# The MoE stage of an attention kernel in six units of 512 tokens in place of eight of 384

## The chip, the cores and the metric

The kernel runs on one core of a Trainium2 chip. The metric is the device time of one execution in microseconds (us): the median of several runs of the kernel. Its engines are named as in the profile: PE is TensorE, PEld its weight loads, DVE VectorE, ACT ScalarE, POOL GpSimd and SP SyncE, which issues the DMAs.

## The reference

A gated linear attention with 4 sequences, 8 heads, 768 tokens and 48 features a head feeds a feed-forward stage with a convolution over the tokens and a gate ("MoE" in the names). The weights of that stage are float64.

```python
f = 1.0 / (1.0 + np.exp(-f_logit))
state = np.zeros((B, H, D, D))
for t in range(S):
    state = f[:, :, t, :, None] * state + np.einsum('bhd,bhe->bhde', k[:, :, t], v[:, :, t])
    y[:, :, t] = np.einsum('bhd,bhde->bhe', q[:, :, t], state)

x = y.transpose(0, 2, 1, 3).reshape(B, S, H * D)           # 4 x 768 x 384
h = np.maximum(x @ w_in, 0.0)                              # 384 -> 1024
conv_out[:, t] = sum(conv_w[k] * hp[:, t + k] for k in range(3))   # hp: h with a row of zeros at both ends
out = (h * sigmoid(conv_out)) @ w_out                      # 1024 -> 384
```

## The kernel before

*Attention.* The 24 chunks (4 sequences of 6 chunks of 128 tokens) are worked one behind the other. For a chunk the logarithms of the gates are summed over its tokens, for the first 9 chunks by matmuls (L556, "cumulate"), later by a scan on DVE (L563); ACT makes exponentials of the sums (L565, L567), and DVE multiplies queries and keys by them (L572, tile `kq`). PE turns the keys (L587, "turn"), which ACT or DVE copies (L598, tile `kp`), and forms the scores (L594); DVE copies them under a causal mask (L602, tile `am`). PE's "rank" (L622 and L614) forms the chunk's two sums for the state and half of its values; DVE adds the sums to the state (L635 half a chunk, L638 a whole one, L642 or L644 the decay); PE's "carry" (L658 and L614) adds what comes from the state. The result lies in PSUM with the heads on partitions in two halves; ACT copies it as the high part of x (L671) and DVE subtracts for the low part (L673, the "x split"), both into `xT`. Each half has 48 features and 16 more columns, which hold a third head: six DMAs per unit on SP's queue (L681, the "gather") move them to rows of their own.

*Weights.* They come as raw 32-bit words (L464) and are split into high and low parts of fp32r by integer and float operations on DVE and ACT; for w_in PE joins parts by four matmuls with 512 columns (L452 to L454).

*The stage with the change, function `moe`.* Before, a unit is half a sequence, 384 tokens; there are 8. For each pair of groups of 128 hidden features:

- L711, PE: nine matmuls with 384 columns (three parts of the 384 inputs, and high × high, high × low, low × high of each) give h in PSUM, in one of two buffers `mm` of 512 columns; "input matmuls", one group of nine per 128 hidden features.
- L721: ReLU with a factor 0.5 into `hb`, a tile in which every group of features has 387 columns: two edge columns to the left, 384, one to the right. L698 clears the edge at a sequence's begin, L701 copies the last two columns of the first half to the left of the second.
- L727, ACT: `g` = middle tap × h; L731, DVE, twice: adds the other taps ("convolution").
- L735, ACT: tanh over both groups; L737, DVE: (tanh + 1) × h, the gate.

The output of the convolution lies one token behind its input, so a unit yields 384 or 385 columns, and a tile of 128 output tokens may need the `g` of two units. For each tile of 128 tokens L754 (ACT) copies `g` as high part `gh`, L758 (DVE) subtracts for the low part `gl`, L767 (PE) makes 16 matmuls with `gh` and 8 with `gl` ("output matmuls", an "output tile"), L773 copies the result from PSUM into `ob`, and L777 writes it out.

*What sets the order.* Every operation is entered with its engine, what it needs and which buffers it takes (`plan.op`), and the order of all of them, over all engines, is a table of numbers written out by hand, ORDER, read by `Plan.fixed`; a number's part behind the dot names the buffer that it takes. Each engine works its list strictly in that order; what comes from another engine is waited for. The operations of attention and of the MoE stage are interleaved by that table: input matmuls of one unit stand between the scores, ranks and carries of the next chunks.

```python
        for w in ORDER.split():
            i, _, k = w.partition(".")
            o = self.ops[int(i.rstrip("v"))]
```

Of the kernel before, what the change touches and what calls it, by code (L numbers as in the profile page):

```python
# [33 lines left out]

ORDER = """
91.0 92 94 95.0 96 97.1 141.0 142.0 2.0 143 3.0 159.1 10.0 160.1 139.0 145 148.0 149.0 689 157.1 140.0 161 144 146.0
147.0 663 8.0 93 98 45.1 46.0 99.0 150 163 166.0 151 164.1 47 165.0 152 48 153 167.1 49 50.0 51 52 177.0 178.0 158.1
168 5.0 23.3 24 100.1 103 104.0 175.2 6.1 179 180 101 105 106.1 162v 109.0 112 25.1 4.0 195.1 196.1 197 169 26 0.0 181
53.0 54 27.0 154 155.0 28 184.0 170 172 213.0 173 29.0 156 214.0 34.0 35 185.0 102 215 107 193.3 176.2 174 36.0 182.0
30.1 113.0 31 183.0 216 32.0 111 199 202.0 186 9.1 200.1 37 203.1 171 187 108.1 33 231.0 38.0 188 211.0 217 190 220.0  # L40
116 229.1 194.0 189 201.0 117.1 198v 40.0 232.0 233 204 11.1 12.3 247.0 7.1 191 39 248.1 221.0 205 55.2 1.0 56 110 114
57.0 192 234 249 115.0 41.1 250 42 60 43.0 13 14.1 206 207 15 17 16.1 283.1 235 212.1 218.0 208 118.1 219.0 222 18.0
120 230.3 119 567 58.0 64 569 568 566 44 209.2 210 564 284.0 285 121 565 690.0 691 19.1 20 59 61 245.2 21.0 22 238.0
236.1 223 237.0 251 65 66.1 69 286v 224 67.1 226 239.1 240 225 62 123.0 125 68 63 664.0 318.2 695.1 281.3 124 287 241
242 254.0 246.0 73.1 336.1 227 122 83 228 676 301 70 665 666.0 71 692 693 243 696 244 82 84.0 255.0 126 252.0 265.0
# [949 lines left out]
```

## Time and profile before

| | us |
|---|---|
| median of the runs | 301.11 (301.06 to 303.17) |
| profiled execution, its own time | 302.57 |
| its span in the trace | 300.7 |

The span is the time from the first to the last recorded instruction; 1.87 us of the execution lie around it. An engine's busy time leaves out DMA issues, semaphores and branches. Matmuls are pipelined and their ends are modelled, so that rows of the timeline overlap, and a busy PE is not PE at its peak; starts of rows are what one subtracts. Each row of the chain is a piece of work, or a wait for it, that something later stood waiting for.

### The profile page before, as it was taken

How to read it: one execution, taken by the hardware profiler on the slowest of the kernel's cores; microseconds unless marked ns; L12 is line 12 of the kernel's file. 1: busy time of each engine (PE TensorE's matmuls, PEld its weight loads, DVE VectorE, ACT ScalarE, POOL GpSimd, SP SyncE). 2: the span in 40 equal slices, each digit the busy share in tenths (PEclk: the TensorE clock that was granted, in tenths of full speed). 3: DMA queues.
4: the chain of work that ended last, by engine and by line, in shares of the span. 5: the costliest groups of instructions: out<-in, count | busy, mean ns of one | idle time of the engine just before them, and what ended most of it. 6: DMA issues, size and time to landing. Idle time of an engine off the chain costs nothing.

```text
span 300.7 us, 10046 instructions
## 1 busy us (share of the span) xinstructions
PE 291.3 (97%) x4319; PEld 274.1 (91%) x4319; DVE 259.6 (86%) x431; ACT 235.7 (78%) x456; POOL 2.8 (1%) x16
## 2 busy tenths in 40 slices
PE   8998979999999999999999999999999999999994
PEld 5777859999999999899999999999999999999994
DVE  4898979999999999989999998989877797399560
ACT  5799869999969699888777799678586896968620
POOL 3000000000000000000000000000000000000000
PEclk9999999999999999999999999999999999999998
DMA  7999688621223126654262165202542612723011
GB/s 229 392 359 349 216 308 295 201 92 28 62 87 108 63 74 238 185 154 128 74 206 85 38 170 171 98 2 66 196 156 66 212 40 59 220 83 122 8 71 59
DMA packets 19269, 43.38 MB, mean 144 GB/s; under 512 B 2685, under 2 KB 10005, under 8 KB 19221
## 3 DMA queue, kind: packets, MB, share of 16 engines
q1 hardware_dynamic: 19076, 42.50, 43.1%
q8 instruction: 35, 0.57, 0.8%
q10 hardware_dynamic: 144, 0.20, 0.2%
q14 instruction: 14, 0.11, 0.1%
HBM read 35.61 MB, written 4.72 MB: 134 GB/s over the span
## 4 chain that ended last, share of the span: by engine, by line
PE 86%; DVE 4%; SPq 3%; DMA 3%; ACT 2%; issue 1%; DVEq 0%; ACTq 0%
PE mm L711 34%; PE mm L767 30%; PE Y L658 3%; PE S L594 3%; PE Y L614 3%; PE Y L622 3%; PE Y L587 3%; PE mm L556 2%; SPq L681 1%; PE mm L452 1%; DMA xT<-xT 1%; DMA v<-in_v_dram 1%; SPq L547 1%; DMA fb<-in_f_token_dram 1%; DVE xT L673 1%
## 5 line engine op out<-in xcount | busy, mean ns | idle before, releaser
L711 PE MATMUL mm<-xT,wi 128*128 128x384 f32 x576 | 107.0, 339 | 1.5 <-DMA xT<-xT 1.5
L711 PEld LDWEIGHTS mm<-xT,wi 128*128 128x128 f32 x576 | 99.3, 188 | 2.9 <-ACT e L567 1.6
L731 DVE SCALAR_TENSOR_TENSOR g<-hb,cw,g 128x385 f32<-128x385 f32 (+1 forms) x128 | 74.5, 616 | 3.8 <-ACT g L727 3.2
L767 PE MATMUL mm<-wo,gh 128*128 128x384 f32 x384 | 70.7, 336 | 0.0
L767 PEld LDWEIGHTS mm<-wo,gh 128*128 128x128 f32 x384 | 66.5, 188 | 0.3
L721 ACT ACTIVATE hb<-mm 128x384 f32<-128x384 f32 x64 | 31.3, 489 | 16.9 <-PE mm L711 16.5
L727 ACT ACTIVATE g<-hb,cw 128x384 f32<-128x384 f32 (+1 forms) x64 | 37.5, 615 | 2.5 <-DVE gl L758 1.9
L767 PE MATMUL mm<-wo,gl 128*128 128x384 f32 x192 | 36.8, 335 | 0.0
L735 ACT ACTIVATE g<-g 128x768 f32<-128x768 f32 (+1 forms) x32 | 26.8, 845 | 9.1 <-DVE g L731 8.9
L572 DVE TENSOR_TENSOR kq<-kq,e 128x1024 f32<-128x1024 f32 x24 | 29.3, 1219 | 5.1 <-ACT e L567 3.4
L767 PEld LDWEIGHTS mm<-wo,gl 128*128 128x128 f32 x192 | 33.5, 188 | 0.0
L754 ACT CAST gh<-g 128x1024 fp32r<-128x1024 f32 (+2 forms) x28 | 26.1, 932 | 9.4 <-PE mm L767 4.5
L758 DVE TENSOR_TENSOR gl<-g,gh 128x1024 fp32r<-128x1024 f32 (+2 forms) x28 | 29.6, 1069 | 3.2 <-PE mm L767 1.9
L737 DVE SCALAR_TENSOR_TENSOR g<-g,hb 128x768 f32<-128x768 f32 (+1 forms) x32 | 30.1, 956 | 0.9 <-ACT g L735 0.7
L614 PE MATMUL Y<-am,v 64*48 64x64 f32 (+1 forms) x768 | 23.5, 220 | 0.0
L602 DVE COPY_PREDICATED am<-mask,S 128x512 f32<-128x512 uint8 x24 | 17.6, 734 | 2.6 <-PE S L594 2.3
L614 PEld LDWEIGHTS Y<-am,v 64*48 64x48 f32 (+1 forms) x768 | 18.7, 127 | 0.0
L563 DVE TENSOR_TENSOR_SCAN fb<-runs,fb 128x512 f32<-128x512 f32 x15 | 18.0, 1218 | 0.3 <-ACT fb L534 0.3
L594 PE MATMUL S<-kq 48*64 48x64 f32 x768 | 16.7, 221 | 0.2 <-DVE kq L572 0.2
L622 PEld LDWEIGHTS Y<-v,kp 64*48 64x48 f32 (+1 forms) x704 | 13.4, 127 | 3.7 <-ACT kp L598 1.3
L622 PE MATMUL Y<-v,kp 64*64 64x48 f32 (+1 forms) x704 | 15.8, 214 | 0.8 <-DMA v<-in_v_dram 0.7
L673 DVE TENSOR_TENSOR xT<-Y,xT 112x512 fp32r<-112x512 f32 x24 | 16.4, 685 | 0.0
(100 smaller groups left out, 341.4 us busy)
## 6 DMA issues: line engine op xcount, KB each, us to landing
kq<-in_kq_dram SPq DMA_DIRECT2D x23, 512.0 KB, 4.8
v<-in_v_dram SPq DMA_DIRECT2D x24, 192.0 KB, 4.1
out_dram<-ob SPq DMA_DIRECT2D x23, 192.0 KB, 3.2
kq<-in_moe_w_in_dram SPq DMA_DIRECT2D x6, 512.0 KB, 4.5
kq<-in_moe_w_out_dram SPq DMA_DIRECT2D x6, 512.0 KB, 4.6
fb<-in_f_logit_dram SPq DMA_DIRECT2D x9, 256.0 KB, 5.0
xT<-xT SPq DMA_DIRECT2D x48, 48.0 KB, 2.3
g<-in_moe_w_in_dram SPq DMA_DIRECT2D x4, 512.0 KB, 6.6
```

The source lines that it names most:

```text
L572: ox = plan.op("DVE", 1222, lambda e, X=X, E=E: nc.vector.tensor_tensor(buf(X), buf(X), buf(E), ALU.mult), ka, need=[o2] + ld_x, use=[X, E])
L614: o = nc.tensor.matmul(out_of(Y, p, j, w, z), buf(V).rearrange("p h d -> p (h d)")[t, h * D:h * D + w], buf(AM)[t, j, p, :], start=x == 1 ...
L622: nc.tensor.matmul(pk(z)[HP * j:HP * j + w, p, :], buf(KP)[t, p, HP * j:HP * j + w], buf(V)[t, 2 * p + j, :], start=True, stop=True)
L711: nc.tensor.matmul(buf(ph)[:, :HS], wi[:, t, wl, f * P:(f + 1) * P], x_view(pl, u)[:, t, xl, :], start=(i == 0), stop=(i == 3 * KT - 1))
L721: nc.scalar.activation(hb[:, 2:HS + 2], buf(ph)[:, :HS], AF.Relu, scale=0.5)
L727: o = pl.op("ACT", 620, lambda e, cv=cv, hb=hb, n=n, f=f: nc.scalar.activation(cv(), hb[:, 1:n + 1], AF.Copy, scale=cw[:, 1, f:f + 1]), ke ...
L731: o = pl.op("DVE", 617, lambda e, cv=cv, hb=hb, n=n, f=f, w=w, sh=sh: nc.vector.scalar_tensor_tensor(cv(), hb[:, sh:n + sh], cw[:, w, f:f ...
L735: o = pl.op("ACT", 846, lambda e, cv=cv: nc.scalar.activation(cv(), cv(), AF.Tanh), key, need=last, use=[("g", u)], mode="T")
L737: gates[u, fp] = pl.op("DVE", 960, lambda e, cv=cv, fp=fp, n=n: nc.vector.scalar_tensor_tensor(cv(), cv(), 1.0, h_b[:, fp:fp + 2, 1:n + 1] ...
L754: o = pl.op("ACT", 180 + 110 * nn * NF // 128, lambda e, hv=hv, src=src: nc.scalar.copy(hv(), src()), key, need=[gates[v, fp] for fp in ra ...
L758: los.append(pl.op("DVE", 150 + 134 * nn * NF // 128, lambda e, hv=hv, lv=lv, src=src: nc.vector.tensor_tensor(lv(), src(), hv().bitcast(F ...
L767: nc.tensor.matmul(buf(po)[:, :DM], view(g)[:, f, :], wo[:, f, wl, :], start=(i == 0), stop=(i == 3 * NF - 1))
```

## The change

A unit is now 512 tokens, and the units run over the ends of sequences: two sequences (1536 tokens) are three units, v = 0, 1, 2. There are 6. The middle one holds the last third of one sequence and the first third of the next, and a zero column is kept between them in `h`.

- `xT` has two buffers of 512 columns instead of three of 384, `g` two of 513 columns for each group of features; `hb` gives way to four tiles `h0` to `h3`, one for each pair of groups, of 2 × 516 columns.
- The tiles of h are allocated when the first unit takes them, on the memory of constants needed only at the start (`stir`, the turned convolution weights, low parts of w_in); `tri32`, `idr` and `negr` lie where `ob` comes later. So the first unit's edge memsets wait for the first unit's gather and for the weights.
- Input matmuls have 512 columns; the ReLU (now always on ACT), the copy, the convolutions, the tanh and the gate likewise 512 or 513 (× 2). An input matmul no longer waits for the gates of the unit before; the edge copies and memsets do, and the ReLU waits for these.
- Three, four and five output tiles follow the three units of a pair of sequences; the output tiles themselves are as before.
- Constants lose their padding, and tiles move: `wi`, `wo`, `gh`, `gl`, `kq`, `v` and the first `xT` begin at 64 modulo 128 bytes (before at 0), the second `xT` at 96, the two `g` at 0 and 32 (as before), the four `h` at 64, 32, 64 and 96.
- ORDER is wholly new.

Line numbers shift by 4 in attention (the x split is L677, the gather L685), by 9 to 10 in the stage: L720 input matmul, L733 ReLU, L741 convolution, L747 gate, L767 `gl`, L776 output matmul, L703 memset of an edge.

```diff
-    HS = S // 2
-    CPH = NC // 2
+    UT = 4 * P
+    CPU = UT // P
+    NU = B * S // UT
-    G1 = HS + 1
+    G1, HW = UT + 1, UT + 4
...
-    h_b = const.tile([P, NF, HS + 3], F32, name="hb")
-    nc.gpsimd.memset(h_b[:, :, HS + 2:], 0.0)
...
+            ring("xT", [P, XW], F32R, [("x", 0), ("x", 1)])
+            ring("low", [P, RW], F32R, [hs[3], hs[2]])
+            ring("c32", [3 * NF, P], F32, hs[:1])
+            pl.ring("z0", [(None, hs[1:2])])
+            pl.ring("tri", [(None, ob[:1])])
+            pl.ring("id", [(None, ob[1:])])
+        for i in range(NF // 2):
+            ring(f"h{i}", [P, 2, HW], F32, hs[i:i + 1])
...
-        for u in range(2 * B):
-            b, hf = u // 2, u % 2
-            n = HS + hf
+        for u in range(NU):
+            b, v = u // 3 * 2, u % 3
+            n, c0 = UT + (v > 0), 1 + (v == 2)
...
+                old, H_ = gates.get((u - 1, fp)), ("h", fp)
+                if v == 0:
+                    oe = pl.op("DVE", 100, lambda e, H_=H_, u=u: [nc.vector.memset(buf(H_)[:, :, i:i + 2], 0.0) for i in ((0,) if u else (0, HW - 2))][-1],
+                               key, need=[old] + (list(x_ready[0][:1]) + W_IN[0] + (W_IN[1] if fp >= 4 else [CW]) if extra and not u else []),
+                               take=[] if u else [(f"h{fp // 2}", H_)], use=[H_] if u else [])
...
-                                nc.tensor.matmul(buf(ph)[:, :HS], wi[:, t, wl, f * P:(f + 1) * P], x_view(pl, u)[:, t, xl, :],
+                                nc.tensor.matmul(buf(ph)[:, :UT], wi[:, t, wl, f * P:(f + 1) * P], x_view(pl, u)[:, t, xl, :],
...
-                    o = pl.op("PE", 1570, mm1, key, need=[gates.get((u - 1, fp))] + list(x_ready[u]) + (W_IN[f // (NF // 2)] if extra else []), use=[("xT", u)],
+                    o = pl.op("PE", 2070, mm1, key, need=list(x_ready[u]) + (W_IN[f // (NF // 2)] if extra else []), use=[("xT", u)],
...
-                    o = pl.op("ACT", 492, relu, key, need=[o, oe], use=[ph])
+                    o = pl.op("ACT", 583, relu, key, need=[o, oe, oz], use=[ph, H_])
...
-            tiles = range(CPH - 1) if hf == 0 else range(CPH - 1, NC)
+            tiles = ((0, 1, 2), (3, 4, 5, 6), (7, 8, 9, 10, 11))[v]
```

Where instructions stand now, at three places, one of SP's queue and two of VectorE's list.

SP's queue at the first unit's gather. Before (L681 is the gather, L464 raw weights, L544 kq, L547 v, L517 gate logits):

```order
L547 DMA v_120<-in_v_dram 128x384
L517 DMA fb_112<-in_f_logit_dram 128x512
L681 DMA xT_340<-xT_340 16x768
L464 DMA g_575<-in_moe_w_out_dram 128x768
L681 DMA xT_340<-xT_340 16x768 x5
L544 DMA kq_115<-in_kq_dram 128x1024
L464 DMA g_575<-in_moe_w_out_dram 128x768
L517 DMA fb_111<-in_f_logit_dram 128x512 x2
L547 DMA v_119<-in_v_dram 128x384
L544 DMA kq_116<-in_kq_dram 128x1024
```

And in the changed order (L685 the gather, L465 raw weights, L548 kq, L551 v, L519 and L521 gate logits):

```order
L521 DMA fb_109<-in_f_logit_dram 128x512
L519 DMA fb_108<-in_f_token_dram 128x384
L521 DMA fb_109<-in_f_logit_dram 128x512 x2
L548 DMA kq_113<-in_kq_dram 128x1024
L685 DMA xT_308<-xT_308 16x1024 x6
L465 DMA raw_813<-in_moe_w_out_dram 128x768
L551 DMA v_114<-in_v_dram 128x384
L465 DMA raw_813<-in_moe_w_out_dram 128x768
L548 DMA kq_110<-in_kq_dram 128x1024
L551 DMA v_115<-in_v_dram 128x384
```

The six gathers stand together now, with a kq load right ahead of them in place of right behind, and with the raw weights behind.

VectorE's list from the fourth x split on. Before, it (L673, `xT_681`, already the second unit's) comes among the weights' splitting (L416, L419, L414, L422), a key product (L572) and state sums (L635, L638); the first memsets of `hb` stand at the list's beginning:

```order
L416 TENSOR_SCALAR gh_674<-g_575 128x768
L673 TENSOR_TENSOR xT_681<-Y_110,xT_681 112x4x128
L419 SCALAR_TENSOR_TENSOR gh_674<-g_575,gh_674 128x768
L635 TENSOR_TENSOR sh_95<-Y_109,st_93 112x192
L572 TENSOR_TENSOR kq_115<-kq_115,e_122 128x1024
L414 TENSOR_SCALAR gl_734<-g_575 128x768
L422 SCALAR_TENSOR_TENSOR gl_734<-gl_734,g_575 128x768
L569 COPY ft_all<-e_121 128x4
L638 TENSOR_TENSOR st_94<-Y_109,sh_95 112x192
L416 TENSOR_SCALAR gh_739<-g_575 128x768
L602 COPY_PREDICATED am_90<-mask_86,S 128x512
```

And in the changed order from the fourth x split (L677, the first unit's last, `xT_308`) to the first memsets of h (L703):

```order
L677 TENSOR_TENSOR xT_308<-Y_107,xT_308 112x4x128
L422 SCALAR_TENSOR_TENSOR mt_599<-mt_599,raw_574 128x768
L606 COPY_PREDICATED am_88<-mask_85,S 128x512
L422 SCALAR_TENSOR_TENSOR mt_577<-mt_577,raw_574 128x768
L416 TENSOR_SCALAR ms_723<-raw_574 128x768
L639 TENSOR_TENSOR sh_94<-Y_106,st_92 112x192
L487 COPY cw<-mm_130 128x24
L425 TENSOR_SCALAR ms_604<-ms_604 128x768
L419 SCALAR_TENSOR_TENSOR ms_723<-raw_574,ms_723 128x768
L642 TENSOR_TENSOR st_93<-Y_106,sh_94 112x192
L427 SCALAR_TENSOR_TENSOR wo<-mt_577,ms_604 128x2x384
L703 MEMSET h_751 128x2x2 x2
```

The memset of `h_751` stands 10 instructions behind the fourth x split; the next rows are the memset of `h_754`, a key product and a masked copy.

VectorE's list where the first stretch of the prediction ends. Before, at the second state sum of chunk 15 (L638, `st_93`; L731 convolutions, L737 a gate, L758 low parts, L602 a masked copy):

```order
L731 SCALAR_TENSOR_TENSOR g_2170<-hb,cw,g_2170 128x385 x4
L572 TENSOR_TENSOR kq_116<-kq_116,e_121 128x1024
L737 SCALAR_TENSOR_TENSOR g_2170<-g_2170,hb 128x770
L731 SCALAR_TENSOR_TENSOR g_2170<-hb,cw,g_2170 128x385 x2
L635 TENSOR_TENSOR sh_96<-Y_110,st_94 112x192
L638 TENSOR_TENSOR st_93<-Y_110,sh_96 112x192
L731 SCALAR_TENSOR_TENSOR g_2170<-hb,cw,g_2170 128x385
L758 TENSOR_TENSOR gl_2402<-g_1646,gh_2173 128x8x127
L758 TENSOR_TENSOR gl_2435<-g_1646,gh_2405 128x1024
L602 COPY_PREDICATED am_90<-mask_86,S 128x512
```

And in the changed order at the copy of the turned keys of chunk 17 (L602, `kp_120`; L606 a masked copy, L741 a convolution, L747 gates, L639 and L642 state sums):

```order
L741 SCALAR_TENSOR_TENSOR g_1961<-h_948,cw,g_1961 128x513
L747 SCALAR_TENSOR_TENSOR g_1961<-g_1961,h_754 128x1026
L747 SCALAR_TENSOR_TENSOR g_1961<-g_1961,h_948 128x1026
L677 TENSOR_TENSOR xT_1941<-Y_107,xT_1941 112x4x128
L639 TENSOR_TENSOR sh_94<-Y_106,st_92 112x192
L767 TENSOR_TENSOR gl_2335<-g_1245,gh_1963 128x8x127
L576 TENSOR_TENSOR kq_112<-kq_112,e_118 128x1024
L767 TENSOR_TENSOR gl_2335<-g_1961,gh_1963 128x8
L642 TENSOR_TENSOR st_93<-Y_106,sh_94 112x192
L606 COPY_PREDICATED am_89<-mask_85,S 128x512
L602 COPY kp_120<-Y_107 128x448
```

The list has reached chunk 17 here, with the gates of the third unit behind it. The rank of chunk 17 on PE (L626) waits for that copy, and from it on PE has the rest of the program: 24 groups of input matmuls, 16 output tiles, 8 carries, 7 ranks, 6 scores and 6 turns. Before, behind the first input matmul of the fifth unit, there are 32, 17, 8, 7, 6 and 7 of them.

## Rows read from the trace of the kernel before

**Rows 1.** The page: busy times of the engines, and the chain's shares by engine.

```profile
PE 291.3 (97%) x4319; PEld 274.1 (91%) x4319; DVE 259.6 (86%) x431; ACT 235.7 (78%) x456; POOL 2.8 (1%) x16
...
PE 86%; DVE 4%; SPq 3%; DMA 3%; ACT 2%; issue 1%; DVEq 0%; ACTq 0%
```

**Rows 2.** The chain in order of time: start us, us, what.

```profile
12.43 0.91 PE mm L556 x8
...
21.81 0.24 PE mm L454
...
39.32 1.83 PE mm L711 x9
...
42.23 0.23 PE mm L454
...
156.21 3.32 PE mm L711 x18
...
163.69 0.39 PE Y L587 x4
...
249.34 1.56 PE mm L711 x9
...
252.29 9.36 PE mm L711 x54
...
296.91 0.48 ACT ob L773
```

**Rows 3.** Busy times by windows; columns after the engines: granted clock, DMA share, GB/s.

```profile
39.32:156.21 116.89, 116.24 (x2025) 109.72 (x2025) 113.44 (x184) 100.26 (x193) 0.00 (x0) 1.00 0.44 143
156.21:296.91 140.70, 140.18 (x1590) 136.91 (x1590) 113.83 (x188) 102.74 (x189) 0.00 (x0) 1.00 0.33 105
41.16:112.20 71.04, 71.04 (x1150) 65.98 (x1153) 70.72 (x116) 62.44 (x125) 0.00 (x0) 1.00 0.39 125
```

**Rows 4.** Timeline of VectorE: start us, us, engine, line, operation.

```profile
151.74 0.95 DVE L737 SCALAR_TENSOR_TENSOR g<-g,hb 128x770 f32<-128x770 f32 x1
152.61 1.27 DVE L731 SCALAR_TENSOR_TENSOR g<-hb,cw,g 128x385 f32<-128x385 f32 x2
...
154.18 0.36 DVE L638 TENSOR_TENSOR st<-Y,sh 112x192 f32<-112x192 f32 x1
```

**Rows 5.** Groups by line: busy us, mean ns of one, idle before.

```profile
L711 PEld LDWEIGHTS mm<-xT,wi 128*128 128x128 f32 x576 | 99.3, 188 | 2.9 <-ACT e L567 1.6 <-ACT hb L721 0.4
L731 DVE SCALAR_TENSOR_TENSOR g<-hb,cw,g 128x385 f32<-128x385 f32 (+1 forms) x128 | 74.5, 616 | 3.8 <-ACT g L727 3.2
...
L758 DVE TENSOR_TENSOR gl<-g,gh 128x1024 fp32r<-128x1024 f32 (+2 forms) x28 | 29.6, 1069 | 3.2 <-PE mm L767 1.9 <-ACT gh L754 1.2
L572 DVE TENSOR_TENSOR kq<-kq,e 128x1024 f32<-128x1024 f32 x24 | 29.3, 1219 | 5.1 <-ACT e L567 3.4 <-DMA kq<-in_kq_dram 1.5 <-ACT ft_all L569 0.2
...
L563 DVE TENSOR_TENSOR_SCAN fb<-runs,fb 128x512 f32<-128x512 f32 x15 | 18.0, 1218 | 0.3 <-ACT fb L534 0.3
L602 DVE COPY_PREDICATED am<-mask,S 128x512 f32<-128x512 uint8 x24 | 17.6, 734 | 2.6 <-PE S L594 2.3 <-PE Y L614 0.3
...
L673 DVE TENSOR_TENSOR xT<-Y,xT 112x512 fp32r<-112x512 f32 x24 | 16.4, 685 | 0.0
...
L569 DVE COPY ft_all<-e 128x4 f32<-128x4 f32 x9 | 1.5, 162 | 0.0
```

**Rows 6.** Line 737, the gate: ns min/median/max, first and last start.

```profile
L737 DVE SCALAR_TENSOR_TENSOR g<-g,hb x32: 946/953/967, 62.0 to 277.1; 128x768 f32<-128x768 f32 x16, 128x770 f32<-128x770 f32 x16
```

**Rows 7.** Timeline of SyncE's queue, the first gather.

```profile
31.50 0.63 SPq L681 DMA_DIRECT2D xT<-xT  x1
32.18 1.24 SPq L464 DMA_DIRECT2D g<-in_moe_w_out_dram  x1
33.46 3.04 SPq L681 DMA_DIRECT2D xT<-xT  x5
```

**Rows 8.** Line 681, the gathers: time from issue to landing.

```profile
DMA to landing us min/median/max: 2.0/2.3/5.3
```

More of the change, by code (lines that the diff above doesn't have):

```diff
@@ L137, in fixed @@
         for w in ORDER.split():
-            i, _, k = w.partition(".")
+            i, *ks = w.split(".")
             o = self.ops[int(i.rstrip("v"))]
             o.on = "DVE" if i[-1] == "v" else next(iter(o.engs))
-            for r, t in o.take:
+            for (r, t), k in zip(o.take, ks):
                 o.spot.append((t, self.rings[r][int(k)][0]))
@@ L310, in gla_moe_kernel @@
     make_identity(nc, ident)
[L311 removed]
+    tri32 = wk.tile([P, P], F32, tag="ob0", name="tri32", bufs=1)
     nc.gpsimd.memset(tri32, 1.0)
@@ L433, in split_f64 @@
                 sf(), pr(0).bitcast(U32), 2.0 ** -52, sf(), ALU.mult, ALU.mult), [s], use=(0, 2))
-            return step("DVE", 150 + 540 * x, lambda e: V.tensor_tensor(hi(), mf(), sf(), ALU.add), [o], use=(1, 2))
+            return plan.op("DVE", 150 + 540 * x, lambda e: V.tensor_tensor(hi(), mf(), sf(), ALU.add), key, need=[o],
+                           use=[ids[1], ids[2]], take=[("c32", "c32")])
         h = step("ACT", 160 + 455 * x, lambda e: A.copy(hi(), parts(mf(), hi())), [m], use=(1,))
@@ L454, in join @@
                 nc.tensor.matmul(to, idr, low()[:, w], start=False, stop=True)
-            j = plan.op("PE", 60 + 675 * x, join, key, need=[h, o], use=[ids[1], ids[3]], take=[("mm", pz)], mode="r", n=8)
+            j = plan.op("PE", 60 + 675 * x, join, key, need=[h, o], use=[ids[1], ids[3], "id"], take=[("mm", pz)], mode="r", n=8)
             done.append(plan.op(dict(ACT=140 + 240 * x, DVE=150 + 265 * x), 0, lambda e, z=z, pz=pz: (
@@ L726, in moe @@
[L726 to L732 removed]
+                    hf = lambda H_=H_, i=f - fp: buf(H_)[:, i]
@@ new lines, in moe @@
+                    cv = lambda u=u, f=f, n=n: g_view(u)[:, f, :n]
+                    o = pl.op("ACT", 711, lambda e, cv=cv, hf=hf, n=n, f=f, c0=c0: nc.scalar.activation(
+                        cv(), hf()[:, c0:n + c0], AF.Copy, scale=cw[:, 1, f:f + 1]), key, need=[o] + ([CW] if extra else []),
+                        take=[("g", ("g", u))] if f == 0 else [], use=[H_] + ([("g", u)] if f else []))
+                    for w, sh in ((2, c0 + 1), (0, c0 - 1)):
+                        o = pl.op("DVE", 750, lambda e, cv=cv, hf=hf, n=n, f=f, w=w, sh=sh: nc.vector.scalar_tensor_tensor(
+                            cv(), hf()[:, sh:n + sh], cw[:, w, f:f + 1], cv(), ALU.mult, ALU.add), key, need=[o], use=[("g", u), H_])
@@ L739, in moe @@
-            tiles = range(CPH - 1) if hf == 0 else range(CPH - 1, NC)
-            for k, m in enumerate(tiles):
-                key = (CPH * (u + 2), "m2", u, k * CPH / len(tiles), "m2d")
+                gates[u, fp] = pl.op("DVE", 1227, lambda e, cv=cv, H_=H_, n=n, c0=c0: nc.vector.scalar_tensor_tensor(
+                    cv(), cv(), 1.0, buf(H_)[:, :, c0:n + c0], ALU.add, ALU.mult), key, need=[o], use=[("g", u), H_])
+            tiles = ((0, 1, 2), (3, 4, 5, 6), (7, 8, 9, 10, 11))[v]
+            for k, q in enumerate(tiles):
+                b, m = u // 3 * 2 + q // NC, q % NC
+                key = (CPU * (u + 2), "m2", u, k * CPU / len(tiles), "m2d")
```

198 lines of the change are left out of this document (88 added, 110 removed), and 32 rows, old and new, of the table ORDER.

## The prediction

> **What bounds the kernel now.** I read the page first. TensorE (PE) is busy 97% of the span and VectorE (DVE) 86%; the chain that ended last runs over PE for 86% of the span [rows 1]. In order of time that chain passes through many engines until the first input matmul at 39.32; from there it is a row of PE blocks, with few breaks, to the last output matmul's end at 296.91, where the last copy takes over [rows 2]. A busy PE is not yet a PE at its peak, so I cut the stretch in two with the busy times by windows: from 39.32 to 156.21 DVE is busy 113.44 of 116.89 us, and 70.72 of 71.04 in the middle of it; from 156.21 to 296.91 DVE has 113.83 of 140.70 and PE 140.18 [rows 3]. My reading: to about 156 us VectorE's in-order list sets the pace and PE stretches its work to it; after that PE does. The tail is 300.7 − 296.91 = 3.79 us (last copy and output DMA), the same in both kernels.
>
> The profiled execution took 302.57 us, 1.46 above the median of 301.11; its span is 300.7. I work in the trace's time and take the difference onto the median.
>
> **The change part by part.** *Input matmuls.* 64 groups of nine 384-column matmuls become 48 groups of nine with 512 columns. A group of nine takes 1.56 us and 54 of them 9.36, 173.3 ns each [rows 2]: 160 ns for 384 columns at the granted clock (1.00, the 2.4 GHz level, [rows 3]) and 13.3 over. With the same 13.3, 512 columns take 226.6 ns and a group 2.04 us. The nearest row with 512 columns, the join of the weights' splitting (L454), took 0.23 and 0.24 us [rows 2], so 2.07 to 2.16 per group. I take 2.05, near the first.
>
> *The PE-led part.* Its last stretch begins, before, with the first matmul of the fifth unit at 156.21 [rows 2]. Behind it stand 32 groups, 17 output tiles (24 matmuls each, also 173.3 ns, so 4.16 us), 8 carries, 7 ranks, 6 scores and 7 turns. In the changed order the same rest, but with 24 groups, 16 tiles and 6 turns, stands behind the rank of chunk 17. So from that rank to the end: 140.70 − 4.16 (a tile) − 0.39 (a turn, [rows 2]) − 0.72 (32 × 1.56 = 49.92 against 24 × 2.05 = 49.20) = 135.43 us. By 2.04 it is 135.2, by 2.16 it is 138.1. Switches between fp32 and fp32r blocks are as many, so I take none.
>
> *The VectorE-led part.* The rank of chunk 17 waits for the copy of the turned keys, which the new order puts on DVE (the third order excerpt); 240 DVE instructions stand up to it. Before, 241 stand up to the state sum of chunk 15 that ended at 154.18 + 0.36 = 154.54 [rows 4]. The two lists are alike but for the following. Consecutive rows overlap by 0.08 us (151.74 + 0.95 − 152.61, [rows 4]), so I count a mean of [rows 5] less 0.08. One more key product (+1.14), one less scan (−1.14), one more masked copy (+0.65) and x split (+0.60), one more pair of state sums (2 × 0.28, +0.56), the key copy itself (+0.57: 448 elements, between the 616 ns of 384 and the 685 of 512). Convolution: 57 of 0.536 go, 48 of 0.667 come, since 128 more elements at 1.04 ns (the step from the gate's 768 elements to the key product's 1024, 953 to 1219 ns, is 1.04 each, [rows 5, 6]) make 616 into 749 ns: 32.0 − 30.6 = +1.5. Gate: 13 of 0.87 go [rows 6], 12 of 1.145 come (1026 elements, 1.22): +2.4. Two more low-part subtractions, one of them in two pieces: +1.2. Four small copies of 0.16 less: −0.3; a few memsets of edge columns I take at nothing. Sum +7.2, so 161.7. Over the whole program the same prices make DVE lighter (128 × 0.536 against 96 × 0.667, 32 × 0.87 against 24 × 1.145: 4.9 us); the new order merely has more of it ahead of this point.
>
> Bounds of the convolution's price: the 512-element x split took 685 ns, which would take 48 × 0.064 = 3.1 us off; in proportion to the columns the 616 ns become 821, 48 × 0.072 = 3.5 us more [rows 5]. I keep 749, from the operation's own row and the slope.
>
> *Idle time of VectorE.* Before, it waited 1.5 us for a kq DMA, issued behind the gathers [rows 5]. The new order issues that load ahead of them (first order excerpt), so I take −1.5. The ACT copy ahead of a convolution cost 3.2 us in all [rows 5]; with units of 512 a pair of groups comes 4.1 us after the last in place of 3.1, and the third unit's convolutions stand close behind their groups: I take +1.0 (between 0 and 3.2). So 161.7 − 1.5 + 1.0 = 161.2.
>
> *First unit.* It now wants four chunks, not three, so its gather starts at VectorE's fourth x split. Before, the first gather issue was at 31.50, behind the third split, the last ended at 33.46 + 3.04 = 36.50, and the first matmul began 2.8 us later [rows 2, 7]. I expect the first matmul near 46 to 47. That is no loss by itself: VectorE has other work meanwhile and is the bound. But its first edge memset now waits for the gather too (the tile of h lies where constants lay). In its queue 10 instructions stand between split and memset (the second order excerpt): four of 768 elements at the gate's 0.87, a masked copy, two state sums, and three short ones, which I estimate at 1.0 together (each between a small copy and a masked one): 3.5 + 0.65 + 0.56 + 1.0 = 5.7 us. The gather needs six issues of 0.6 [rows 7] and 2.3 (the median, [rows 8]) to 2.8 for landing: 5.9 to 6.4 us. Stall 0.2 to 0.7, which I leave inside the +1.0 above. Behind the memset are queued a key product and a masked copy, for which PE's scores and rank wait.
>
> *ScalarE, buffers, addresses.* ACT gets fewer and longer instructions and holds 2% of the chain [rows 1]; I price it at nothing, hidden by DVE's fuller list, at most the 3.2 us already bounded. Two x buffers in place of three cost nothing as long as the output tiles behind the last attention block (three, 12.5 us) cover the last gather (six issues and 2.3, about 7 with the split).
>
> *Sum.* 161.2 + 135.4 = 296.6 against 296.91: −0.3 us. Break-even is a rank of chunk 17 at 161.5. Forecast 301.11 − 0.3 = **300.8 us**, no change that can be told (about 1% of 301 is what a measurement of this kernel can tell, so 298.1 to 304.1 is "the same").
>
> **Rivals.** (1) *The weight load sets the 384-column spacing.* Each matmul loads its own weights, and such a load lasts 188 ns [rows 5], more than the 173.3 between two matmuls. If the 13.3 ns are the load's, 512 columns hide it: 216 ns, 1.94 per group, 24 × 0.11 = 2.6 us less behind the rank, and some 0.5 ahead of it, where PE's blocks end a stretch: 300.8 − 3.1 = 297.7, faster. Against it: eight 128-column matmuls with loads of their own took 0.91 us, 114 ns each [rows 2], so a load doesn't need 173 ns; and the 512-column joins show 230 to 240.
> The Trainium skill, page "TensorE: Matmul & The Clock Gate", section "Back-to-back issue gap", says that isolated matmuls follow each other in N/2.4 + 2.5 ns, 215.7 for 512 columns. This trace disagrees at 384 columns: by the formula 162.5, by the row 173.3. By that rule the 48 groups would take 93.2 us, where the sum above has 98.4, and rival 1 would come to the same spacing.
>
> (2) *Slower: the memset stalls VectorE.* Gathers have landed as late as 5.3 us after issue [rows 8], and the new ones carry a third more. Then the last lands 3.6 + 5.3 = 8.9 us behind the split and the memset stalls 8.9 − 5.7 = 3.2 us; with one more issue of SP's as slow as the raw load between the gathers before (1.24, [rows 7]) it is 4.4. VectorE is the bound, so all of it is paid, less the 0.7 that the forecast holds already: 300.8 + 3.7 = 304.5. It decides from a landing over 2.8 us behind the last issue. For it: DVE had 0.3 us of idle in 71 [rows 3], no slack to win it back. Against it: the raw load that stood between the gathers stands behind them now.
>
> (3) *The change doesn't do what it says.* Not all operands lie at one place modulo 128 bytes: the buffers of x are at 64 and 96. And place may not matter: the gate reads two g buffers at different places, and its 32 instructions spread from 946 to 967 ns only [rows 6]. 32 × 0.02 is 0.7 us; the time would be the forecast's, 300.8, by the sizes alone. So this rival moves no chance.
>
> **How the numbers follow.** Forecast 0.46; rival 1, with a cheaper convolution as its fellow (−3.1 by the 512-element x split), 0.28; rival 2, with the dearer 512-column group (+2.7 by 2.16) as its fellow, 0.26. The cases of one side end at 296 to 298, those of the other at 303.4 to 305; both priced together would give 294.6 or 307, which I leave out. Range 296 to 305. Rival 1 alone with 297.7 is beyond −1%: 0.28 faster. Of the slower cases 304.5 is just beyond +1% and 303.4 is not, yet stalls sum, so 0.25 slower and 0.47 the same.
>
> **What would show it.** Right: nine 512-column matmuls start to start in 2.04 to 2.16 us; the first of them at 46 to 47; VectorE over 97% busy to about 160; the rank of chunk 17 at 161.2 ± 1.5; 135 us from it to the last matmul's end; DVE's convolution near 749 ns. Wrong: a group of 1.95 (rival 1); over 2 us idle on VectorE in front of the edge memset (rival 2); convolutions near 685; or PE waiting in the last 100 us, where the forecast has it full.

## The result, and the profile after

The changed kernel takes 305.7 us (median of 6, 305.21 to 307.29), the kernel before beside it on the same chip 302.0 (6, 301.06 to 303.17): a ratio of 1.0128 [1.0092, 1.0164], 1.3% slower. The forecast was 300.8 with a range of 296 to 305. The profiled execution took 305.34 us, its span is 303.5.

The page of the changed kernel, busy times and the chain's shares by engine:

```profile
PE 293.7 (97%) x4175; PEld 256.6 (85%) x4175; DVE 256.3 (84%) x397; ACT 232.6 (77%) x413; POOL 2.7 (1%) x15
...
PE 83%; ACT 7%; DVE 4%; DMA 3%; issue 2%; ACTq 0%; DVEq 0%; SPq 0%
```

Against [rows 1], PE has 2.4 us more work, though the same products are formed by 144 fewer matmuls, and VectorE has 3.3 us less. The time went to PE. The chain of the changed kernel, start us, us, what (first around the rank of chunk 17, then its end):

```profile
161.28 1.42 PE mm L776 x8
162.70 0.42 PE Y L626 x9
...
230.81 12.87 PE mm L776 x72
243.68 16.86 PE mm L720 x72
260.54 36.62 PE mm L776 x208
297.27 1.62 PE mm L776 x8
298.91 0.48 ACT ob L782
```

72 input matmuls in 16.86 us are 234 ns each, 2.11 us for a group of nine; 208 output matmuls in 36.62 are 176.1 ns, 4.23 us for a tile of 24. The forecast had 2.05 and 4.16. The two stretches of the forecast, from the first input matmul and from the rank of chunk 17 (columns as in [rows 3]):

```profile
45.97:162.70 116.73, 115.83 (x1850) 100.25 (x1852) 112.30 (x169) 102.67 (x189) 0.00 (x0) 1.00 0.45 136
162.70:298.91 136.21, 136.18 (x1490) 123.52 (x1490) 104.75 (x156) 93.89 (x148) 0.00 (x0) 1.00 0.35 105
```

The granted clock is 1.00 in both, so no level of the clock takes part. PE is as full as the forecast said behind the rank, and every wait there would show as a gap between 136.21 and 136.18. What is dearer are the matmuls themselves. VectorE's groups, its list around the first unit and at the copy of the turned keys of chunk 17 (the last line), and SyncE's queue:

```profile
L741 DVE SCALAR_TENSOR_TENSOR g<-h,cw,g 128x513 f32<-128x513 f32 (+1 forms) x96 | 69.5, 746 | 6.1 <-ACT g L737 5.5
...
L747 DVE SCALAR_TENSOR_TENSOR g<-g,h 128x1026 f32<-128x1026 f32 (+1 forms) x24 | 28.8, 1218 | 1.8 <-ACT g L745 1.8
```

```profile
44.42 0.96 DVE L427 SCALAR_TENSOR_TENSOR wo<-mt,ms 128x768 fp32r<-128x768 f32 x1
45.33 1.23 DVE L576 TENSOR_TENSOR kq<-kq,e 128x1024 f32<-128x1024 f32 x1
45.33 0.10 DVE L703 MEMSET h<- 128x4 f32 x4
...
161.50 0.61 DVE L602 COPY kp<-Y 128x448 f32<-128x448 f32 x1
```

```profile
39.74 5.04 SPq L685 DMA_DIRECT2D xT<-xT  x6
```

The six gathers are issued by 39.74 + 5.04 = 44.78, VectorE's list runs on from 44.42 + 0.96 = 45.38 into the memsets without a gap, and the first input matmul starts at 45.97. The copy for which the rank of chunk 17 waits ends at 161.50 + 0.61 = 162.11, 0.59 before that rank begins; until then PE is still at an output tile.

The end of the program, by the last output's transfer: KB, and us from its issue to its landing, before and after:

```profile
out_dram<-ob ACTq DMA_DIRECT2D x1, 192.0 KB, 1.9
```

```profile
out_dram<-ob ACTq DMA_DIRECT2D x1, 192.0 KB, 2.4
```

### The profile page after: what moved, and what is told of

The parts are those of the page before. It is cut to its first block, busy times and chain, and to the rows that moved or that the text cites. A ratio compares the mean times of both kernels' runs of the same rounds, so it can differ in the third digit from the quotient of the medians.

```text
span 303.5 us, 9661 instructions
## 1 busy us (share of the span) xinstructions
PE 293.7 (97%) x4175; PEld 256.6 (85%) x4175; DVE 256.3 (84%) x397; ACT 232.6 (77%) x413; POOL 2.7 (1%) x15
## 4 chain that ended last, share of the span: by engine, by line
PE 83%; ACT 7%; DVE 4%; DMA 3%; issue 2%; ACTq 0%; DVEq 0%; SPq 0%
PE mm L776 32%; PE mm L720 31%; PE S L598 3%; PE Y L626 3%; PE Y L618 3%; PE Y L662 3%; PE Y L591 3%; DMA fb<-in_f_logit_dram 3%; PE mm L560 2%; PE mm L381 2%; DVE g L747 2%; ACT fb L534 1%; PE S L381 1%; PE mm L453 1%; ACT fb L538 1%
## 5 line engine op out<-in xcount | busy, mean ns | idle before, releaser
L720 PE MATMUL mm<-xT,wi 128*128 128x512 f32 x432 | 107.0, 400 | 0.2 <-issue 0.2
L720 PEld LDWEIGHTS mm<-xT,wi 128*128 128x128 f32 x432 | 79.6, 188 | 18.4 <-issue 0.3
L741 DVE SCALAR_TENSOR_TENSOR g<-h,cw,g 128x513 f32<-128x513 f32 (+1 forms) x96 | 69.5, 746 | 6.1 <-ACT g L737 5.5
L776 PE MATMUL mm<-wo,gh 128*128 128x384 f32 x384 | 71.5, 339 | 0.2 <-ACT gh L763 0.2
L776 PEld LDWEIGHTS mm<-wo,gh 128*128 128x128 f32 x384 | 67.5, 188 | 1.1 <-ACT gh L763 0.5
L733 ACT ACTIVATE h<-mm 128x512 f32<-128x512 f32 x48 | 28.4, 595 | 14.4 <-PE mm L720 13.8
L776 PE MATMUL mm<-wo,gl 128*128 128x384 f32 x192 | 38.2, 342 | 0.0
L767 DVE TENSOR_TENSOR gl<-g,gh 128x1024 fp32r<-128x1024 f32 (+2 forms) x28 | 29.6, 1066 | 7.0 <-ACT gh L763 5.7
L737 ACT ACTIVATE g<-h,cw 128x513 f32<-128x513 f32 (+1 forms) x48 | 34.1, 722 | 0.7
L776 PEld LDWEIGHTS mm<-wo,gl 128*128 128x128 f32 x192 | 33.5, 188 | 0.4
L576 DVE TENSOR_TENSOR kq<-kq,e 128x1024 f32<-128x1024 f32 x24 | 29.1, 1218 | 5.5 <-ACT e L571 4.9
L747 DVE SCALAR_TENSOR_TENSOR g<-g,h 128x1026 f32<-128x1026 f32 (+1 forms) x24 | 28.8, 1218 | 1.8 <-ACT g L745 1.8
L745 ACT ACTIVATE g<-g 128x1026 f32<-128x1026 f32 (+1 forms) x24 | 25.2, 1059 | 6.3 <-DVE g L741 6.2
L677 DVE TENSOR_TENSOR xT<-Y,xT 112x512 fp32r<-112x512 f32 x24 | 16.2, 680 | 4.6 <-ACT xT L675 4.6
L675 ACT CAST xT<-Y 112x512 fp32r<-112x512 f32 x24 | 13.9, 583 | 7.2 <-PE Y L618 7.2
L606 DVE COPY_PREDICATED am<-mask,S 128x512 f32<-128x512 uint8 x24 | 17.6, 734 | 1.9 <-PE S L598 1.7
L626 PEld LDWEIGHTS Y<-v,kp 64*48 64x48 f32 (+1 forms) x704 | 13.7, 127 | 4.7 <-issue 2.9
L626 PE MATMUL Y<-v,kp 64*64 64x48 f32 (+1 forms) x704 | 16.3, 215 | 0.8 <-issue 0.5
```

Of the source, the lines that this page charges most:

```text
L576: ox = plan.op("DVE", 1222, lambda e, X=X, E=E: nc.vector.tensor_tensor(buf(X), buf(X), buf(E), ALU.mult), ka, need=[o2] + ld_x, use=[X, E])
L626: nc.tensor.matmul(pk(z)[HP * j:HP * j + w, p, :], buf(KP)[t, p, HP * j:HP * j + w], buf(V)[t, 2 * p + j, :], start=True, stop=True)
L720: nc.tensor.matmul(buf(ph)[:, :UT], wi[:, t, wl, f * P:(f + 1) * P], x_view(pl, u)[:, t, xl, :], start=(i == 0), stop=(i == 3 * KT - 1))
L733: nc.scalar.activation(to, of, AF.Relu, scale=0.5)
L737: o = pl.op("ACT", 711, lambda e, cv=cv, hf=hf, n=n, f=f, c0=c0: nc.scalar.activation(cv(), hf()[:, c0:n + c0], AF.Copy, scale=cw[:, 1, f: ...
L741: o = pl.op("DVE", 750, lambda e, cv=cv, hf=hf, n=n, f=f, w=w, sh=sh: nc.vector.scalar_tensor_tensor(cv(), hf()[:, sh:n + sh], cw[:, w, f: ...
```

## The experiments

Three questions: what made the matmuls dearer (the runs up to the map moved by 32 bytes), whether the forecast's sum holds without that (the run at distance 0), and which engine sets the pace ahead of the rank of chunk 17 (the rest). Where a run has a single time, only its profile is used.

An address here is a tile's place in a partition, in bytes, as the kernel's allocation gives it. Of a matmul's two operands one is loaded into PE as its weights and one streams through: an input matmul loads `wi` and streams x, an output matmul loads gh or gl and streams `wo` (in `mm<-wo,gh 128*128 128x384` the 128*128 are what is loaded, the 128x384 what streams). For each kind of matmul there is also a *distance*: the address of the streamed operand less that of the loaded one, modulo 512. Steps inside these tiles are multiples of 512 bytes, so that one number holds for all matmuls on a buffer. Before, all distances are 0. In the changed kernel they are 384 for the first x buffer (even units), 416 for the second (odd units), and 128 for the output matmuls.

**All operands to 0 modulo 128.** On the changed kernel:

```diff
-    cw = const.tile([P, 3, NF], F32, name="cw")
+    cw = const.tile([P, 3 * NF + 16], F32, name="cw")[:, :3 * NF].rearrange("p (k f) -> p k f", k=3)
-            ring(f"h{i}", [P, 2, HW], F32, hs[i:i + 1])
+            ring(f"h{i}", [P, 2, HW + (0 if i else 12)], F32, hs[i:i + 1])
```

> The changed kernel with two paddings (64 bytes ahead of w_in's tile, 96 behind the first tile of h), so that w_in, w_out, both x buffers, gh and gl begin at 0 modulo 128 bytes, as before the change; the order is not touched. Theory PLACE (a matmul whose operands begin at 64 or 96 modulo 128 is slower): in pure stretches the output matmul goes from 176 back to 173.3 ns and the 512-column matmul from 234 to about 227 ns (13.3 over the 213.3 of its columns); behind the rank of chunk 17 that is 24 x 9 x 7 ns + 16 x 24 x 2.8 ns = 2.6 us less, over the whole program at most 4.6 us less: 301 to 303 us, ratio to the kernel before 0.997 to 1.004. Rival WIDTH (512 columns cost 234 ns by themselves, and the output matmuls are slowed by the new neighbours on other engines): 234 and 176 ns stay, ratio 1.013.

304.58 us (303.58 to 304.95, 6) against 301.81 (17), ratio 1.0096 [1.0073, 1.0119]. Its chain: three groups of unit 3 (second x buffer, distance now 0), three of unit 4 (first buffer, 384), the eight of unit 5 (distance 0), and output matmuls (128):

```profile
164.06 6.36 PE mm L720 x27
...
217.98 6.47 PE mm L720 x27
...
242.11 16.42 PE mm L720 x72
258.53 36.58 PE mm L776 x208
```

At one place modulo 128 the output matmuls still take 36.58 / 208 = 175.9 ns; only the input matmuls of the odd units became cheaper, 16.42 / 72 = 228 ns, and the three groups of unit 3 take 6.36 us where the three of unit 4 take 6.47. So the theory of the place falls. What the cheap ones have in common with those of before is the distance 0.

**The kernel before with everything at 64 modulo 128.**

```diff
-    ones = const.tile([P, 17], F32, name="ones")[:, :1]
+    ones = const.tile([P, 1], F32, name="ones")
```

> The kernel before with 64 bytes of padding taken out (the tile of ones), so that w_in, w_out, the x buffers, gh and gl all begin at 64 modulo 128 bytes; nothing else. Theory PLACE: the 384-column matmuls, input and output, go from 173.3 to about 176 ns in pure stretches; 32 x 9 + 17 x 24 = 696 of them stand behind 156 us, so 1.9 us, at most 1152 x 2.8 ns = 3.2 us more: ratio to the kernel before 1.006 to 1.011. Rival WIDTH: 173.3 ns and ratio 1.000.

302.19 us (301.36 to 305.06, 12), ratio 1.0029 [1.0005, 1.0053]. Its chain keeps the spacing of before away from 0, 9.36 / 54 = 173.3 ns as in [rows 2] and 26.40 / 152 = 173.7:

```profile
251.48 9.36 PE mm L711 x54
...
265.17 26.40 PE mm L767 x152
```

**One operand alone.** The weights to 0 modulo 128 (the padding of `cw` as above, and 16 columns behind `wo`), or x, gh and gl to 0 (the padding of the first h, and the same 16 columns):

```diff
-    far = const.tile([P, n_w], F32, name="far")
+    far = const.tile([P, n_w + 16], F32, name="far")[:, :n_w]
```

> The changed kernel with w_in and w_out alone at 0 modulo 128; x (64 and 96), gh and gl (64) stay where the change put them. In an input matmul the columns that stream are x and the loaded weights are w_in; in an output matmul w_out streams and gh or gl is loaded. PLACE by the streaming operand: output matmul 173.3 ns, input matmul stays at 232 to 234. PLACE by the loaded operand: output stays at 176, input goes to about 227. WIDTH: both stay.

> The reverse: x, gh and gl at 0 modulo 128, w_in and w_out stay at 64. PLACE by the streaming operand: input matmul about 227 ns, output matmul stays at 176. PLACE by the loaded operand: input stays at 232 to 234, output 173.3. WIDTH: both stay.

304.01 and 302.55 us, one time each. The chain of the first, three groups of unit 4, unit 5 and output tiles:

```profile
218.62 6.50 PE mm L720 x27
...
242.61 16.80 PE mm L720 x72
259.40 36.12 PE mm L776 x208
```

And of the second:

```profile
241.90 16.61 PE mm L720 x72
258.50 36.11 PE mm L776 x208
```

In both the output matmuls are back at 173.6 ns, whichever operand was moved; in both their distance is 64. Input matmuls of unit 5 take 233 ns at a distance of 480 (the first) and 231 at 64 (the second); the three groups of unit 4, at 448, take 6.50 us, no less than the 6.47 at 384. Neither operand is at fault by itself; how the two stand to each other decides. 64 is about as good as 0 for both kinds, 448 and 480 are not, so the pattern is finer than "0 or not".

**Distance 0, places kept.** On the changed kernel; all operands stay at 64 modulo 128, the order of every engine is untouched:

```diff
+            for i in (1, 0):
+                pool.tile([P, XW], F32R, tag=f"x{i}", name=f"x{next(serial)}", bufs=1)
-    far = const.tile([P, n_w], F32, name="far")
+    far = const.tile([P, n_w + 32], F32, name="far")[:, :n_w]
```

> The changed kernel with 128 bytes of padding behind w_out and the two x buffers allocated side by side: all matmul operands still begin at 64 modulo 128, but the loaded and the streaming operand of every input and output matmul now lie a multiple of 512 bytes apart (before the change they do too; in the changed kernel 384 and 416 apart modulo 512). Order untouched. Theory DISTANCE (the spacing depends on how far apart, modulo 512, the two operands lie, not on the place modulo 128): output matmul 173.3, 512-column matmul 227 in all units; 432 x 6 + 576 x 2.8 ns = 4.2 us less if PE sets all of the time, 2.7 if only behind the rank of chunk 17: 301.5 to 303, ratio to before 0.997 to 1.004. Rival ORDER (new neighbours on other engines, distance plays no part): 176 and 232 to 234 stay, ratio 1.010 to 1.013.

302.69 us (301.97 to 303.73, 12) against 301.83 (17), ratio 1.0031 [1.0012, 1.0050]; the changed kernel's was 1.0128. Lines are 2 further on. Its chain:

```profile
159.93 1.44 PE mm L778 x8
161.37 0.42 PE Y L628 x9
...
241.59 16.47 PE mm L722 x72
258.06 36.16 PE mm L778 x208
...
295.99 0.48 ACT ob L784
```

228.8 and 173.8 ns. The rank of chunk 17 starts at 161.37 (forecast 161.2), and from there to the last matmul's end it is 134.62 us (forecast 135.43).

**The kernel before at a distance of 384.**

```diff
-    far = const.tile([P, n_w], F32, name="far")
+    far = const.tile([P, n_w + 96], F32, name="far")[:, :n_w]
```

> The kernel before with 384 bytes of padding behind w_out, so that streaming and loaded operands lie 384 apart modulo 512 in place of 0; every operand stays at 0 modulo 128, nothing else changes. DISTANCE: the 384-column matmuls go from 173.3 to about 176 ns, 1152 x 2.8 = 3.2 us at most, 1.9 behind 156 us alone: ratio to before 1.006 to 1.011. ORDER: 173.3 stays, ratio 1.000.

304.62 us (302.8 to 305.56, 5), ratio 1.0115 [1.0076, 1.0154]: 384 bytes of padding, and nothing else, cost the kernel before about as much as the whole change. The distance is 384 for x and 128 for the output matmuls. Its chain, from the fifth unit's first matmul:

```profile
155.19 3.37 PE mm L711 x18
...
252.04 9.50 PE mm L711 x54
...
265.94 26.76 PE mm L767 x152
...
297.27 0.48 ACT ob L773
```

And the kernel before without the padding, its last output tiles:

```profile
265.99 26.40 PE mm L767 x152
```

9.50 / 54 = 175.9 and 26.76 / 152 = 176.1 ns, against 173.3 [rows 2] and 173.7. By these rows its 576 + 576 matmuls cost 576 × 2.6 + 576 × 2.4 = 2.9 us more; the ratio says 3.5 [2.3, 4.6].

**A map of distances.** On the kernel before, 64 bytes behind each buffer of x, gh and gl, so that the buffers differ. As distances, streamed less loaded, x is at 0, 64 and 128, gh at 320 and 256, gl at 192 and 128; the expectation below counts gh and gl the other way round, as buffer less weights:

```diff
-            x = new("xT", [P, XW], F32R, 3)
+            x = new("xT", [P, XW + 16], F32R, 3)
...
-        pl.ring("gh", [(new("gh", [P, RW], F32R, 2), [("gx", i)]) for i in (0, 1)])
-        pl.ring("gl", [(new("gl", [P, RW], F32R, 2), [("gx", i)]) for i in (2, 3)])
+        pl.ring("gh", [(new("gh", [P, RW + 16], F32R, 2), [("gx", i)]) for i in (0, 1)])
+        pl.ring("gl", [(new("gl", [P, RW + 16], F32R, 2), [("gx", i)]) for i in (2, 3)])
```

> The kernel before with 64 bytes of padding behind each of the buffers of x, gh and gl: the distance to the weights becomes 0, 64 and 128 for the three x buffers, 192 and 256 for gh, 320 and 384 for gl (modulo 512), so one profile maps the spacing of the 384-column matmul over the distance. DISTANCE: 173.3 at 0, about 176 at 384, others between 173 and 178 by distance. ORDER: 173.3 at all seven.

One time, 304.14. PE's timeline there, one tile (start us, us, the rest as before):

```profile
277.19 2.93 PE L767 MATMUL mm<-wo,gh 128*128 128x384 f32 x16
279.95 1.57 PE L767 MATMUL mm<-wo,gl 128*128 128x384 f32 x8
281.37 2.94 PE L767 MATMUL mm<-wo,gh 128*128 128x384 f32 x16
```

Start to start, sixteen with gh take 2.76 us, 172.5 ns each, and eight with gl 1.42, 177.5: in one tile, with the same `wo` streaming, the buffer of the loaded operand decides. gh (320, 256) is cheap, gl (192, 128) dear. x takes 173 ns at 0 and 64, 175 at 128.

**The map moved by 32 bytes.** The same with 8 columns behind `wo`; x is then at 32, 96 and 160, gh at 288 and 224, gl at 160 and 96:

```diff
-    far = const.tile([P, n_w], F32, name="far")
+    far = const.tile([P, n_w + 8], F32, name="far")[:, :n_w]
```

> The kernel of the first map with everything behind w_out another 32 bytes on: streaming address minus loaded address becomes 32, 96 and 160 modulo 256 for the three x buffers, 32 and 224 for the two gh, 160 and 96 for the two gl. The seven distances so far fit one rule: clean (173.3 ns) where streaming minus loaded lies from 0 up to below 128 modulo 256, slow (175 to 176) from 128 to 255. By this rule (HALF) 32 and 96 are clean and 160 and 224 slow. Rival RULE-512 (the pattern repeats only every 512, with other borders): some of 32 and 96 slow or some of 160 and 224 clean.

One time, 301.54 (before beside it 300.85). Its chain, unit 7 (distance 96) and output tiles:

```profile
250.81 9.54 PE mm L711 x54
...
264.72 26.63 PE mm L767 x152
```

96 costs 9.54 / 54 = 176.7 ns; 32 is uneven, 171 to 176; 160 is cheap, 174. gl takes 174 at 160 and 177 at 96, like x there. That breaks the rule put forward for this run: a half of every 256 that is good and one that is bad doesn't describe it. The exact pattern stays open; 0 was cheap in every run. But with the distance counted as streamed less loaded, one list serves both kinds of matmul: at 64, 96, 128 and 160 both were measured with 384 columns, and they are cheap, dear, dear and cheap alike.

**Which engine sets the pace ahead of the rank.** All on the kernel with distance 0. VectorE relieved: the convolutions of units 0 to 2 on 64 columns in place of 512 or 513 (the rest of the convolution is left out). PE relieved: input matmuls of units 0 to 2 without the product of the weights' low part, 6 of 9. The check on the other half: convolutions of units 3 to 5 on 64 columns. Last, both reliefs together.

```diff
-                        o = pl.op("DVE", 750, lambda e, cv=cv, hf=hf, n=n, f=f, w=w, sh=sh: nc.vector.scalar_tensor_tensor(
+                        o = pl.op("DVE", 750, lambda e, cv=cv, hf=hf, n=64 if u < 3 else n, f=f, w=w, sh=sh: nc.vector.scalar_tensor_tensor(
-                            cv(), hf()[:, sh:n + sh], cw[:, w, f:f + 1], cv(), ALU.mult, ALU.add), key, need=[o], use=[("g", u), H_])
+                            cv()[:, :n], hf()[:, sh:n + sh], cw[:, w, f:f + 1], cv()[:, :n], ALU.mult, ALU.add), key, need=[o], use=[("g", u), H_])
...
-                            for wl, xl in ((0, 0), (0, 1), (1, 0)):
+                            for wl, xl in ((0, 0), (0, 1), (1, 0))[:NM(u)]:
...
+    def NM(u):
+        return 2 if u < 3 else 3
```

For the other half the first condition is `u >= 3`.

> On the kernel with distance 0 (e5): the convolutions of the first three units work on 64 columns in place of 512 or 513 (the rest of the convolution is left out there), 48 instructions of about 0.2 in place of 0.67 us: some 21 us less for VectorE ahead of the rank of chunk 17, which in e5 begins at 161.4 us. Theory VECTOR (VectorE's list sets the pace until then, as the prediction had it): that rank comes at least 3 us earlier, until PE's own work binds, and the end by as much, since PE needs 134.6 us from there. Rival TENSOR (PE sets it there too): the rank moves by under 0.7 us.

> On e5: the input matmuls of the first three units leave out the part with w_in's low half, 6 matmuls per group in place of 9: 24 x 3 x 0.227 = 16 us less for PE ahead of the rank of chunk 17. VECTOR: that rank moves by at most 1 us from 161.4. TENSOR: it comes 5 us or more earlier.

> On e5: the convolutions of the last three units on 64 columns (the rest left out there), some 21 us less for VectorE behind the rank of chunk 17. Both theories hold that PE alone binds there: the stretch from that rank to the last matmul stays at 134.6, within 0.7 us. If it shrinks by more than 1 us, VectorE binds there as well.

> On e5, both reliefs at once: in the first three units the convolutions on 64 columns and the input matmuls without w_in's low part (the rest left out there). Alone each moved the rank of chunk 17 by 0.5 and 1.0 us. Theory BOTH (PE and VectorE are each nearly full until then, so that relieving one hands over to the other): together the rank comes at least 4 us earlier, 157 or before. Rival THIRD (a third thing, ScalarE or the transfers, sets the pace): it moves by under 1.5 us.

Times, one each: 301.87, 303.22, 302.17 (before beside them 303.12) and 299.32 (before 300.85). Busy times in two windows ahead of the rank, with distance 0 and no relief:

```profile
45.50:100.00 54.50, 54.20 (x877) 44.90 (x869) 54.38 (x85) 50.96 (x98) 0.00 (x0) 1.00 0.47 154
128.00:161.40 33.40, 33.40 (x526) 29.04 (x525) 31.26 (x50) 26.68 (x46) 0.00 (x0) 1.00 0.35 98
```

With VectorE relieved, and the rank in that kernel's chain:

```profile
45.50:100.00 54.50, 54.16 (x886) 45.02 (x876) 44.23 (x93) 50.88 (x98) 0.00 (x0) 1.00 0.47 155
```

```profile
160.92 0.42 PE Y L628 x9
```

With PE relieved:

```profile
45.50:100.00 54.50, 46.70 (x833) 36.09 (x824) 53.87 (x84) 50.80 (x98) 0.00 (x0) 1.00 0.46 153
```

```profile
160.38 0.42 PE Y L628 x9
```

With both:

```profile
45.50:100.00 54.50, 48.37 (x905) 38.38 (x908) 44.27 (x92) 52.58 (x105) 0.00 (x0) 1.00 0.46 151
```

```profile
155.70 0.42 PE Y L628 x9
```

Ten us less work on VectorE in the first window bring the rank forward by 161.37 − 160.92 = 0.45 us; seven and a half less on PE by 0.99; both together by 5.67. By the words put down ahead the first run speaks for TENSOR, the second for VECTOR and the third for BOTH. The first two moves are no larger than the scatter of that rank over versions with the same work (161.36 to 162.70); the third is. Neither engine alone sets the pace there: the other is nearly as full and takes over at once. With both relieved ACT is the fullest in that window, 52.58 of 54.50. The check on the other half, behind the rank, without and with VectorE relieved:

```profile
161.40:296.00 134.60, 134.55 (x1490) 122.54 (x1490) 104.47 (x156) 93.91 (x149) 0.00 (x0) 1.00 0.35 106
```

```profile
161.40:296.00 134.60, 134.44 (x1490) 122.62 (x1488) 83.26 (x156) 94.12 (x149) 0.00 (x0) 1.00 0.35 106
```

21 us less on VectorE move nothing there; the last copy starts at 295.88 in place of 295.99. Behind the rank PE binds alone.

## Why the prediction was wrong

**The step that failed** is the price of the matmuls: "With the same 13.3, 512 columns take 226.6 ns and a group 2.04 us", and the output tile at 4.16 unchanged. Both rest on [rows 2], rows of a kernel whose operands lie at a distance of 0 modulo 512, and the diff's new addresses were not priced on PE at all. In the changed kernel a group takes 2.11 and a tile 4.23. At distance 0 the step measured right: 16.47 / 8 = 2.06 a group, 36.16 / 208 × 24 = 4.17 a tile. The prediction's upper price for a group, 2.16 from the joins of L454, covered the 2.11, but it rode on rival 2 and gave no cause; for the output tile there was no second price.

**What it costs.** 432 × (16.86 − 16.47) / 72 = 2.3 us for the input matmuls and 576 × (36.62 − 36.16) / 208 = 1.3 for the output matmuls, 3.6 together. The ratios of the two versions differ by 0.0097 of 302, 2.9 us (by their intervals some 1.2 either way), and account for that much of the 3.9 by which the change is slower (0.0128 of 302). From the rank to the last matmul's end, PE's own stretch, the profiles give 136.21 against 134.62, 1.6; the kernel before gives 140.70, with the distance at 384 142.08 (297.27 − 155.19), 1.4. Ahead of the rank profiles scatter: the run with all operands at 0 modulo 128 had its rank at 161.36 with most of its matmuls still dear, so the 162.70 of the changed kernel isn't put down to the distance alone.

**Rival 3 looked at the right thing and priced it on the wrong engine.** It saw that addresses change and took the gate's spread on VectorE [rows 6] as proof that place doesn't matter. Place doesn't matter much on PE either (ratio 1.0029 at 64 modulo 128); the distance of a matmul's two operands does. No row of the trace of before could show it, since all its distances are alike; it was an unknown cost to be bounded from both sides.

The Trainium skill, page "TensorE: Matmul & The Clock Gate", section "Step-by-step: what each phase is for", says that PE has two independent read ports, one for the streamed operand and one for the weights: "Loading the next tile's weights doesn't steal SBUF read bandwidth from the running matmul." By that the place of one operand against the other should not show in the time. Here it does: the spacing of 384 columns is 173.3 or 176 ns by the relative address of the two. By what path, no run shows.

**Rival 1 is refuted.** It had 512 columns at 216 ns; the least a run showed is 228, distance 0, 15 above the 213 ns of 512 columns. The overhead of 13.3 at 384 columns is nearly the same at 512.

**Rival 2 is refuted, and it rested on a misreading.** The memset stood behind no wait: it follows its neighbours at 45.33. By the diff it needs `list(x_ready[0][:1])`, the first of the six gathers alone, and not the last, as the prediction and the section on the change have it. The first was issued at 39.74, 5.6 us before VectorE came to the memset; its pieces landed 2.5 us after the issue. The last was issued at 44.19 and landed 2.4 us later, behind the memset: had the memset needed it, VectorE would have stood still for over 1 us. First matmul at 45.97, forecast 46 to 47.

**VectorE's rows held:** convolution 746 ns (forecast 749), gate 1218 (1.22); it was busy for 112.30 of 116.73 us, 96%, where over 97% was forecast. But "to about 156 us VectorE's in-order list sets the pace and PE stretches its work to it" was wrong as a cause. In the changed kernel's chain the rank follows an output tile's matmuls without a gap (161.28 + 1.42 = 162.70), 0.59 us after VectorE's copy, and the reliefs show two engines nearly full. The 161.2 that came from summing VectorE's list was right within 0.2 at distance 0 because both lists end at about the same time; that PE's list, which was not summed, ends there too is luck.

**PE-led part right:** 134.62 at distance 0 against 135.43, and there VectorE relieved by 21 us changes nothing.

**Tail:** "the same in both kernels" was wrong by 0.5 to 0.8 us. It is 303.5 − 298.91 = 4.59 in the changed kernel and 300.3 − 295.99 = 4.31 at distance 0, against 3.79 before; all versions with the new order had 4.3 to 4.9, all with the old one 3.8. The traces show where it lies. From its issue the last output lands in 1.9 us in every version with the old order and in 2.1 to 2.8 with the new one (2.4 in the changed kernel, 2.2 at distance 0), and from that landing to the last instruction it is 1.38 us with the old order and 1.65 with the new one. Nothing was tried on either, so the cause is open. At distance 0 this is half of the 0.9 us that the change still costs.

**The level.** The sum's −0.3 us was taken onto a median from a profiled execution that stood 1.46 above it. That is a large part of the miss. In the trace's own time the forecast was 296.6 + 3.79 = 300.4 us and the span measured 303.5: 1.5 us at the rank, 0.8 from there to the last matmul's end, 0.8 in the tail. The other 1.8 of the 4.9 us between 300.8 and 305.7 are the step from a span to a median, taken as 300.8 − 300.4 = 0.4 us and measured as 305.7 − 303.5 = 2.2. The 301.11 was the median of three runs; with three more it is 302.0. By profiled executions the change at distance 0 is 0.5 faster than before (302.05 against 302.57), by the ratio 0.3% slower; one profiled execution is not good to half a per cent. The forecast's case, no change that can be told, is what the version at distance 0 does. None of the versions that do the whole work is faster than the kernel before by more than the noise.

## What to carry to other kernels

When a change moves tiles, compare the addresses of each matmul's streamed and loaded operands with each other, modulo 512 bytes, not each with a boundary: on a kernel bound by PE a pad behind one tensor was worth 1%. Count streamed less loaded, and look up in the kernel which operand is which. A price read from rows holds only for the addresses it was read at; where the diff changes an address, bound that on the engine that binds. And where two engines are both over 95% busy, as ahead of the rank here, relieving one can give back little: 0.5 and 1.0 us alone, 5.7 together.
